# First batch's steps in another order, zero products between them, and another token layout for keys and v

## The chip, the cores and the metric

The kernel runs on one core of one Trainium2 chip. The metric is the device time of one execution in microseconds (us). Engines are named as in the profile: PE is TensorE (PEld its weight loads), DVE is VectorE, ACT is ScalarE, POOL is GpSimd, SP is SyncE. Each engine works through its own list of instructions in order and waits on semaphores for the others. SP issues the loads of q and k, POOL those of v and of the weights.

## What is computed

The reference is an attention with normalised q and k, followed by a two-layer network with a tanh-GELU; batch is 8, heads 12, sequence 448, head size 64, d_model 768, d_ff 2048.

```
def rmsnorm(x, g):
    rms = np.sqrt(np.mean(x * x, axis=-1, keepdims=True) + 1e-06)
    return x / rms * g
q_n, k_n = (rmsnorm(q, g_q), rmsnorm(k, g_k))
scores = scale * np.matmul(q_n, k_n.transpose(0, 1, 3, 2))
attn = np.exp(scores - np.max(scores, axis=-1, keepdims=True))
attn = attn / (np.sum(attn, axis=-1, keepdims=True) + 1e-09)
attn_out = np.matmul(attn, v)
x = attn_out.transpose(0, 2, 1, 3).reshape(B * S, H * D)
h = x @ w_in
g = 0.5 * h * (1.0 + np.tanh(c * (h + 0.044715 * h * h * h)))
out = g @ w_out
```

## The kernel before

**Tiling.** A batch's 12 heads are worked on as six pairs `hp`; two pairs with the same `c = hp // 2` are loaded together (a load chunk `(b, c)`, halves `j = hp % 2`). A chunk brings q of four heads with four tokens in a row on 112 places (partitions) and k of the same heads. The 448 keys of a head are cut into 3 tiles of 128 keys and a rest of 64. The rests of two heads share one tile: slot `NK = 3` of the seven slots of `rawk`, where head half 0 owns places 0 to 63 and head half 1 places 64 to 127 (`own(j)`). Of v the 3 full tiles lie in `vb`, the rests in `vr`, whose other half is zero. There is one `vb` and one `vr` for even and one for odd batches.

**Steps of a chunk.** Squares of q and k (`sq`, `sk`), their sums (`tq`, `tk`, DVE), the inverse root (`rs`, a Ln and an Exp on ACT), the normalised q and k (`nq`, `nk`), transposes on PE (`tpq`, `tpk`), and their copies to SBUF (`cq`, `ck`). A letter after a colon names the engine (A is ACT, D is DVE, P is POOL). Then for each of 21 score tiles the scores (`s0` to `s20`, PE) and their exponential (`e0` to `e20`, ACT, into `ex` or, for a tile of rests, `exr`); for each pair the sums over keys (`sa`, `sb`, PE with `ones`), the reciprocals (`st`, `rc`, `rb`, DVE), the product with v (`xa`, `xb`, PE) and its scaling (`xt`, DVE). `v0`, `v1`, `v2` are the v loads of batch 0, `V0` to `V2` those of batch 1, `w` and `o` the loads of the two weights, `L11` and `L12` load chunks of batch 1, all queued on POOL or SP at the place where they stand. Capital letters are steps of batch 1.

**What sets the order.** For the first batch the order is written out by hand in the string `FRONT`; `front()` issues one step after the other, and each engine sees its own steps in that order. The `mb`, `ma`, `mc`, `md` steps are the first network layer (`mm1`) of batch 0, `g` its GELU. Later batches run in a loop in which the scores of batch b+1 lie between the second-layer products (`mm2`) of batch b; this loop is not part of the change, except for the loads and the v products that it calls. The step `y` issues products of zeros with 224 columns and `z` such with 448 (`idle`), whose results nothing reads; the kernel begins with 20 of the latter. Score tiles have two places in PSUM, and a third after step `U`.

## Time and profile before

| | |
|---|---|
| median of 3 runs | 413.26 us (412.65 to 413.44) |
| the profiled execution's own time | 413.83 us |
| its span, first to last instruction | 412.1 us |
| mean granted TensorE clock | 0.992 |
| PE busy | 403.7 us (98%) |
| ACT, DVE, POOL busy | 296.2, 274.3 and 131.8 us |
| DMA moved | 54.21 MB in 97870 packets |

Busy time is the time in which an engine has an instruction in it. Matmuls overlap, so that PE can be busy while a matmul that could start is late. Idle time before an instruction is given in brackets with what ended it. The `PEclk` rows give the share of full clock that TensorE was granted.

### The profile page before, as it was taken

The page shows a single profiled execution, that of the slowest core. Times are in us where ns is not written, and L with a number is a line of the kernel's source. Part 1 is how long each engine was busy: PE and PEld are TensorE (multiplying, and loading weights), DVE is VectorE, ACT ScalarE, POOL GpSimd, SP SyncE. Part 2 cuts the span into 40 slices and gives each one's busy share as a digit, 9 for nine tenths or more (in the row PEclk, how much of TensorE's full clock was granted, in tenths as well). Part 3 has the DMA queues.
Part 4 walks back from the last instruction along what each step waited for, and adds up shares of the span by engine and source line. Part 5 has one row for each costly group of instructions (what it writes and reads, how often), then busy time and mean ns, then how long its engine had stood idle before and what let it go on. Part 6 is the DMA issues. An engine that isn't in the chain of part 4 may idle for free.

```text
span 412.1 us, 10085 instructions
## 1 busy us (share of the span) xinstructions
PE 403.7 (98%) x4207; PEld 243.5 (59%) x4207; DVE 274.3 (67%) x454; ACT 296.2 (72%) x398; POOL 131.8 (32%) x144
## 2 busy tenths in 40 slices
PE   8799999999999999999999999999999999999996
PEld 3344555566655666557655666556655575556664
DVE  4899739899899638884678747786488633783010
ACT  5797987969988587767977778785976558774300
POOL 7689000234500942037500745019310460000000
PEclk9699999999999999999999999999999999999999
DMA  8999995999981689229981399616991161210022
GB/s 191 227 235 228 203 196 141 227 227 192 213 145 38 139 176 207 66 52 176 222 140 41 78 203 171 136 40 145 171 145 40 23 112 40 72 46 2 2 77 78
DMA packets 97870, 54.21 MB, mean 132 GB/s; under 512 B 63776, under 2 KB 94368, under 8 KB 97824
## 3 DMA queue, kind: packets, MB, share of 16 engines
q1 hardware_dynamic: 71392, 41.69, 43.4%
q0 software_dynamic: 26112, 11.80, 22.5%
q8 instruction: 33, 0.54, 0.6%
q10 hardware_dynamic: 320, 0.07, 0.1%
q14 instruction: 13, 0.11, 0.1%
HBM read 45.61 MB, written 11.01 MB: 137 GB/s over the span
## 4 chain that ended last, share of the span: by engine, by line
PE 95%; SPq 2%; DMA 1%; DVE 0%; ACT 0%; issue 0%; ACTq 0%; DVEq 0%
PE o L441 36%; PE hh L412 31%; PE o L370 11%; PE sc L324 8%; PE h L412 5%; PE sc L310 1%; DMA rawq<-in_q_dram 1%; PE ox L370 1%; SPq L143 1%; SPq L118 1%; SPq L136 1%; PE tp L245 0%; PE o L477 0%; PE tp L238 0%; ACT ex L331 0%
## 5 line engine op out<-in xcount | busy, mean ns | idle before, releaser
L441 PE MATMUL o<-wout,g 128*64 128x384 bf16 (+1 forms) x1648 | 160.6, 327 | 0.0
L331 ACT ACTIVATE ex<-sc,shift 128x896 bf16<-128x896 f32 x144 | 136.1, 1011 | 1.3 <-PE sc L324 1.3
L412 PE MATMUL hh<-xT,win 128*64 128x448 bf16 (+1 forms) x1260 | 133.8, 353 | 0.0
L441 PEld LDWEIGHTS <-g 128*64 128x64 bf16 (+1 forms) x1648 | 96.2, 109 | 58.3 <-issue 14.8
L412 PEld LDWEIGHTS <-win 128*64 128x64 bf16 (+1 forms) x1440 | 95.4, 109 | 49.9 <-issue 3.2
L421 ACT ACTIVATE g<-hh 128x896 bf16<-128x896 f32 x56 | 50.1, 919 | 44.5 <-PE hh L412 44.4
L203 DVE TENSOR_REDUCE ss<-sq 128x14 f32<-128x896 f32 (+4 forms) x45 | 47.9, 1080 | 32.4 <-ACT sq L186 19.9
L454 ACT COPY osb<-o 128x384 f32<-128x384 f32 x50 | 24.2, 483 | 47.8 <-PE o L441 47.8
L788 POOL COPY mark<-es 1x1 bf16<-1x1 bf16 x8 | 1.8, 225 | 162.9 <-DVE es L345 158.5
L377 DVE STREAM_TRANSPOSE st<-o 128x448 f32<-128x448 f32 x48 | 31.1, 648 | 23.6 <-PE o L370 23.2
L324 PE MATMUL sc<-qT,kT 64*128 64x448 bf16 (+1 forms) x372 | 39.6, 360 | 1.7 <-DVE kT L264 1.3
L345 DVE TENSOR_TENSOR es<-ex 128x896 bf16<-128x896 bf16 x42 | 26.8, 637 | 12.0 <-ACT ex L331 12.0
L226 POOL TENSOR_TENSOR nrmq<-rawq,rinv 112x512 bf16<-112x512 f32 x33 | 34.0, 1043 | 0.0
L226 POOL TENSOR_TENSOR nrmk<-rawk,rinv 128x512 bf16<-128x512 f32 (+1 forms) x33 | 31.1, 957 | 4.2 <-ACT rinv L212 4.2
L385 DVE STREAM_TRANSPOSE rb<-rc 128x448 f32<-128x448 f32 x48 | 31.0, 645 | 1.6
L370 PE MATMUL o<-ex,vb 128*64 128x448 bf16 x252 | 30.9, 352 | 0.0
L279 DVE TENSOR_SCALAR kT<-kT,gcol 128x896 bf16<-128x896 bf16 x19 | 21.1, 1108 | 11.7 <-DMA kT<-nrmk 11.7
L343 DVE TENSOR_TENSOR es<-es,exr 64x896 bf16<-64x896 bf16 x42 | 25.9, 617 | 2.4 <-ACT exr L331 1.0
L345 DVE TENSOR_TENSOR es<-es,ex 128x896 bf16<-128x896 bf16 x42 | 25.5, 608 | 2.3 <-ACT ex L331 0.3
L395 DVE TENSOR_TENSOR xT<-o,rb 128x448 bf16<-128x448 f32 x42 | 25.8, 615 | 1.4 <-PE o L370 0.9
L188 POOL TENSOR_TENSOR sq<-rawq 112x1024 f32<-112x1024 f32 x9 | 17.0, 1893 | 28.4 <-DMA rawq<-in_q_dram 25.0
L324 PEld LDWEIGHTS <-kT 64*128 64x128 bf16 (+1 forms) x372 | 10.9, 99 | 24.6 <-issue 18.1
(83 smaller groups left out, 349.4 us busy)
## 6 DMA issues: line engine op xcount, KB each, us to landing
rawq<-in_q_dram SPq DMA_DIRECT2D x48, 224.0 KB, 4.4
rawk<-in_k_dram SPq DMA_DIRECT2D x48, 192.0 KB, 4.6
vb<-in_v_dram POOLq DMA_DIRECT2D x8, 576.0 KB, 10.1
win<-in_moe_w_in_dram POOLq DMA_DIRECT2D x4, 768.0 KB, 14.1
wout<-in_moe_w_out_dram POOLq DMA_DIRECT2D x4, 768.0 KB, 20.4
out_dram<-osb SPq DMA_DIRECT2D x7, 336.0 KB, 4.3
out_dram<-osb SPq DMA_DIRECT2D x8, 288.0 KB, 2.7
out_dram<-osb SPq DMA_DIRECT2D x8, 240.0 KB, 2.6
```

The source lines that it names most:

```text
L203: nc.vector.reduce_sum(stat(ssq[b % 3], b, c, n, j), view(n, sqs[n, b, c], j), axis=AX.X)
L226: eng.tensor_mul(dst.rearrange("p t a d -> p a t d"), view(n, raws[n, b, c], j), r.to_broadcast(list(r.shape) + [D]),)
L324: nc.tensor.matmul(sc[o, a, :S], kT[r, c, 4 * j + t, o], qT[b][r, hp], start=True, stop=True,)
L331: nc.scalar.activation(dst, sc[:, :, :S], AF.Exp, scale=scale, bias=shift)
L343: nc.vector.tensor_add(es[p], es[p], exrs[b, hp // 2][p])
L345: nc.vector.tensor_add(es, ex[:, 0] if t == 1 else es, ex[:, t])
L370: nc.tensor.matmul(o[a * D:(a + 1) * D], w(a), e[:, a], start=(i == 0), stop=(i + 1 == len(steps)),)
L377: nc.vector.transpose(oas["st"].rearrange("p a b -> p (a b)"), oas[0])
L385: nc.vector.transpose(oas["rb", hp], oas["rc"].to_broadcast([128, S // 32, 32]))
L412: nc.tensor.matmul(h[i * m:(i + 1) * m, j, :S], win[:, c // 2 + NCH * (c % 2), f * 128 + i * m:f * 128 + (i + 1) * m], xT[b][:, c], start= ...
L421: nc.scalar.activation(g[:, fs[0]:fs[0] + len(fs), (b % 2) * S:(b % 2 + 1) * S], hs1[fs[0]][:, :, :S], AF.Gelu_apprx_tanh)
L441: nc.tensor.matmul(o[j * m:(j + 1) * m, :HD], g[:, f, i * 128 + j * m:i * 128 + (j + 1) * m], wout[:, f, half * HD:(half + 1) * HD], start ...
```

## The change

Three things change together. First, k and v of a head are laid out anew: the first 256 tokens lie four in a row on the head half's own 64 places, the other 192 three in a row on the other 64 places. Slot 3 holds the fourth tokens of the own places, so that score tiles keep their shapes. A chunk's k comes in four transfers to 64 places each, where there were two to 128 places and two small ones to 64, and in another order. `vr` is gone: `vb` has a fourth slot, whose unused half is set to zero, and a batch's v comes in four transfers to 64 places instead of one to 128 and two small ones. The step `v0` now issues two transfers, `v1` and `v2` one each. Second, the order in `FRONT` changes, and some steps change their engine (`nk1` goes from DVE to POOL, `sq4` from POOL to ACT; of batch 1, `Sk2` and `Sq2` leave ACT for POOL and DVE, `Cq0` and `Ck0` change places between ACT and DVE, and `Sk1` stands ahead of `e20`). `v0` and `w0` are issued later, after the square `sk4`. Third, zero products are put into `FRONT`: `y4`, `z3`, `y3`, `z3`, `z1`, `y4`, `z1`, that is 11 of 224 columns and 8 of 448, where there was one `y3`.

```diff
@@ -93,8 +93,8 @@
     win = wts.tile([128, HP, d_ff], BF16)
     wout = wts.tile([128, nf, d_model], BF16)
 
-    vb = [wts.tile([128, H, NK, D], BF16, name=f"vb{i}") for i in range(2)]
-    vr = [wts.tile([128, 2, HP, D], BF16, name=f"vr{i}") for i in range(2)]
+
+    vb = [wts.tile([128, H, NK + 1, D], BF16, name=f"vb{i}") for i in range(2)]
     ones = consts.tile([128, D], BF16)
     onesr = consts.tile([128, 2, D], BF16)
     kT = consts.tile([128, NCH, NS, 128], BF16)
@@ -111,9 +111,13 @@
     def head(c, j):
         return 2 * c + HP * j
 
+    def raw_q(b, c):
+        if ("q", b, c) not in raws:
+            raws["q", b, c] = rawqk.tile([P, CH, NQ, D], F32, tag="rawq", name="rawq")
+        return raws["q", b, c]
+
     def load_q(b, c):
-        t = rawqk.tile([P, CH, NQ, D], F32, tag="rawq", name="rawq")
-        raws["q", b, c] = t
+        t = raw_q(b, c)
         return [
             lambda j=j: nc.sync.dma_start(
                 t[:, 2 * j:2 * j + 2],
@@ -122,7 +126,10 @@
             for j in range(2)
         ]
 
-    SM = 128 * NK
+    SM = 64 * (NK + 1)
+
+    def keys(j, n):
+        return (own(j), slice(0, SM)) if n > NK else (own(1 - j), slice(SM, S))
 
     def own(j):
         return slice(64 * j, 64 * j + 64)
@@ -131,33 +138,29 @@
         t = rawqk.tile([128, 2, NS, D], F32, tag="rawk", name="rawk")
         raws["k", b, c] = t
 
-        def main(j):
+        def part(j, n):
+
+            at, span = keys(j, n)
+            s = slice(NK * j + j * (n == NK), NK * j + j * (n == NK) + n)
             h = head(c, j)
             nc.sync.dma_start(
-                t[:, :, 4 * j:4 * j + NK],
-                k[b, h:h + 2, :SM].rearrange("a (p t) d -> p a t d", t=NK),
+                t[at, :, s], k[b, h:h + 2, span].rearrange("a (p t) d -> p a t d", t=n)
             )
-
-        def last(j):
-            h = head(c, j)
-            nc.sync.dma_start(t[own(j), :, NK], k[b, h:h + 2, SM:].rearrange("a p d -> p a d"))
-        return [lambda: main(0), lambda: main(1), lambda: last(0), lambda: last(1)]
+        return [lambda j=j, n=n: part(j, n) for j in range(2) for n in (4, 3)]
 
     def loads(b, c):
         lq, lk = load_q(b, c), load_k(b, c)
-        for go in (lq[0], lk[0], lq[1], *lk[1:]):
+        for go in (lq[0], *lk[:2], lq[1], *lk[2:]):
             go()
 
     def load_v(b, part):
-        if part == 0:
+
+        for j, n in ((0, NK), (1, NK)) if part == 0 else ((part - 1, NK + 1),):
+            at, span = keys(j, n)
+            first = j * (n == NK)
             nc.gpsimd.dma_start(
-                vb[b % 2].rearrange("p h t d -> p h (t d)"),
-                v[b, :, :SM].rearrange("h (p t) d -> p h (t d)", t=NK),
-            )
-        else:
-            j = part - 1
-            nc.gpsimd.dma_start(
-                vr[b % 2][own(j), j], v[b, HP * j:HP * j + HP, SM:].rearrange("h p d -> p h d")
+                vb[b % 2][at, HP * j:HP * j + HP, first:first + n].rearrange("p h t d -> p h (t d)"),
+                v[b, HP * j:HP * j + HP, span].rearrange("h (p t) d -> p h (t d)", t=n),
             )
 
     def view(n, t, j=None):
@@ -355,8 +358,12 @@
         o = oas[what]
         main = [exs[b, hp][:, t] for t in range(NK)]
         if what:
-            steps = [(main[t], lambda a, t=t: vb[b % 2][:, head(c, j) + a, t]) for t in range(NK)]
-            steps.append((exrs[b, c], lambda a: vr[b % 2][:, j, 2 * c + a]))
+            steps = [
+                (e, lambda a, t=t: vb[b % 2][:, head(c, j) + a, t])
+                for t, e in enumerate(main[:NK * (1 - j)] + [exrs[b, c]] + main[:NK * j])
+            ]
+            if j:
+                steps.append(steps.pop(0))
         elif b == 0:
             steps = [(e, lambda a: ones) for e in main] + [(exrs[b, c], lambda a: onesr[:, j])]
         else:
@@ -605,7 +612,6 @@
     nc.scalar.preload_act_table_set(EXP_SET)
     loads(0, 1)
     loads(0, 2)
-    loads(1, 0)
     nc.vector.memset(eps, 1e-6)
     nc.vector.memset(ones, 1.0)
     nc.vector.memset(rows, 1.0)
@@ -614,7 +620,8 @@
     for j in range(2):
         nc.gpsimd.memset(onesr[own(j), j], 1.0)
     for i in range(2):
-        nc.gpsimd.memset(vr[i], 0.0)
+        for j in range(2):
+            nc.gpsimd.memset(vb[i][own(1 - j), HP * j:HP * j + HP, NK * (1 - j)], 0.0)
     for i in range(1, 3):
         nc.gpsimd.memset(ssq[i], 1.0)
 
@@ -732,6 +739,9 @@
             w_out_part(i // 2, slice(i % 2 * nf // 2, (i % 2 + 1) * nf // 2))
         elif name == "L":
             loads(*divmod(i, 10))
+        elif name == "H":
+
+            eng.memset(raw_q(*divmod(i, 10))[:1, 0, 0, :1], 0.0)
         elif name in ("Sq", "Sk"):
             square(1, i, n, eng)
         elif name in ("Tq", "Tk"):
@@ -759,18 +769,18 @@
             raise ValueError(step)
 
     FRONT = """
-        sq0:A sk0:P gcol tq0 tk0 sq1:P rs0 sk1:A nq0:P v1 nk0:D shift tq1 tk1 sq2:A tpq0 tpk0 v2
-        v0 sk2:A rs1 sq3:A cq0:D ck0:D tq2 s0 e0 y3 s1 nk1:D nq1:D L11 e1 tpk1 tpq1 s2 sk3:P w0
-        tq3 tk2 rs2 e2 ck1:D cq1:D s3 e3 sa0 s4 sk4:P tk3 nq2:D nk2:D rs3 tpk2 tpq2 s5 sb0 tk4
-        ck2:D cq2:D nq3:D st0 e4 nk3:P e5 s6 sk5:P L12 e6 tpk3 tpq3 s7 e7 s8 sa1 s9 sb1 xa0 e8
-        sq4:P sq5:P w1 rc0 cq3:D rb0 ck3:D tq4 tk5 rs4 e9 xb0 s10 st1 xt0 rc1 rb1 tq5 e10 sa2
-        s11 e11 rs5 nk4:P nq4:P w2 nk5:P nq5:P xa1 xb1 sb2 s12 e12 s13 tpk4 tpq4 xt1 st2 ck4:D
-        cq4:D rc2 xa2 e13 rb2 sa3 xb2 s14 tpk5 tpq5 s15 e14 xt2 ck5:D cq5:D sb3 e15 U s16 s17
-        xa3 xb3 s18 w3 o0 Sk0:P e16 st3 rc3 rb3 e17 xt3 e18 s19 sa4 xa4 sb4 xb4 Tk0 st4 rc4 s20
-        mb0 mb1 mb2 mb3 sa5 e19 e20 o1 Sq0:P Sq1:P V0 rb4 GELU xt4 Tq0 xa5 sb5 xb5 st5 V1 V2 o2
-        o3 Sk1:A rc5 rb5 ma1 mc0 mc1 xt5 md0 ma2 md1 mc2 md2 Tq1 Tk1 g0 EXP md3 Rs0 g1 Nk00:D
-        Nq11:D Nq00:D Tp0 md4 Cq0:A g2 Sq2:A g3 Nk10:D Nk01:D Nq01:D Ck0:D Tp1 md5 Sk2:A Tq2 Tk2
-        Nk11:D Nq10:D Ck1:A g4 Cq1:A g5 md6 md7 g6 g7 md8 g8
+        L10 sq0:A gcol tq0 sk0:P tk0 rs0 sq1:P sk1:A nq0:P nk0:D v1 tq1 shift tk1 sq2:A y4 tpk0
+        tpq0 z3 v2 sk2:A rs1 sq3:A ck0:D cq0:D s0 e0 s1 nq1:D nk1:P L11 e1 tpq1 y3 s2 tpk1 z3
+        sk3:P tq3 tq2 cq1:D tk2 ck1:D e2 rs2 z1 s3 e3 tk3 nk2:D nq2:D rs3 s4 y4 z1 sa0 s5 tpq2
+        sb0 tpk2 nq3:D st0 cq2:D ck2:D e4 sk4:P v0 nk3:P e5 s6 sk5:P w0 sq5:P w1 L12 e6 sa1 tpq3
+        s7 s8 tpk3 sb1 sq4:A e7 s9 xa0 e8 tk4 rc0 cq3:D rb0 ck3:D st1 rc1 tq4 e9 rs4 xb0 s10 xt0
+        rb1 tq5 tk5 e10 sa2 s11 xa1 xb1 e11 rs5 w2 nq4:P nk4:P nq5:P nk5:P sb2 tpq4 s12 s13 tpk4
+        xt1 st2 e12 cq4:D rc2 ck4:D xa2 e13 rb2 xb2 sa3 s14 tpq5 tpk5 e14 xt2 cq5:D ck5:D s15
+        sb3 e15 U s16 s17 xa3 xb3 s18 w3 Sk0:P e16 st3 rc3 rb3 e17 xt3 e18 s19 sa4 sb4 xa4 xb4
+        s20 Tk0 st4 rc4 mb0 mb1 mb2 mb3 sa5 e19 Sk1:A o0 o1 Sq0:P Sq1:P V0 V1 rb4 e20 GELU xt4
+        Tq0 xa5 sb5 xb5 st5 V2 o2 o3 Sk2:P rc5 rb5 mc0 ma1 mc1 xt5 md0 ma2 md1 mc2 md2 Tk1 Tq1
+        g0 EXP md3 Rs0 g1 Nk00:D Nq00:D Nq01:D Tp0 md4 Sq2:D Ck0:A g2 Tq2 Cq0:D Nk11:D g3 Nk10:D
+        Nk01:D Nq11:D Tk2 Nq10:D g4 md5 Tp1 g5 Ck1:A Cq1:A md6 md7 g6 g7 md8 g8
 """
     for step in FRONT.split():
         front(step)
```

## The prediction

> **What bounds the kernel now.** I read the page first: the span, the shares of the engines, and the clock by slices (tenths of full clock in 40 equal slices of 10.3 us).
>
> ```profile
> span 412.1 us, 10085 instructions
> ...
> PE 403.7 (98%) x4207; PEld 243.5 (59%) x4207; DVE 274.3 (67%) x454; ACT 296.2 (72%) x398; POOL 131.8 (32%) x144
> ...
> PEclk9699999999999999999999999999999999999999
> ```
>
> PE is the bound with 98% of the span, and its clock is short in the second slice alone (the 6), which is where the change is. I therefore asked for busy time by stretches; the stretches are those of the granted clock (columns: busy time and count of PE, PEld, DVE, ACT, POOL, then granted clock, DMA share, GB/s).
>
> ```profile
> 7.18:14.00 6.82, 4.33 (x34) 2.05 (x32) 6.10 (x13) 4.71 (x8) 6.05 (x7) 1.00 1.22 228
> 14.00:20.83 6.83, 6.05 (x37) 2.45 (x36) 5.57 (x13) 5.67 (x9) 4.03 (x5) 0.50 1.37 230
> 20.83:27.66 6.83, 6.42 (x63) 2.96 (x62) 6.72 (x15) 6.51 (x11) 5.45 (x6) 1.00 1.17 243
> 27.66:34.49 6.83, 6.83 (x63) 3.12 (x60) 6.29 (x13) 6.53 (x8) 6.80 (x7) 1.00 1.20 227
> ```
>
> From 7.18 to 14.00 PE was busy for 4.33 of 6.82 us (63%); in the 6.83 us behind that the clock was 0.50. After 20.83 it is full again, and PE is nearly always busy. So two things cost time: waits before 14, and half clock up to 20.83. The timeline of PE shows both (start, us, instruction, and in brackets the idle time before it).
>
> ```profile
> 8.13 0.93 PE L217 MATMUL w<-zeros 128*128 128x448 bf16 x4
> ...
> 10.73 0.36 PE L324 MATMUL sc<-qT,kT 64*128 64x448 bf16 x2 [1.30 <-DVE kT L264]
> 11.02 0.46 PE L217 MATMUL w<-zeros 128*128 128x224 bf16 x3
> 11.42 0.36 PE L324 MATMUL sc<-qT,kT 64*128 64x448 bf16 x2
> ...
> 13.36 0.37 PE L238 MATMUL tp<-ident,nrmq 112*128 112x112 bf16 x4 [1.05 <-DVE nrmq L226]
> ...
> 14.80 0.88 PE L310 MATMUL sc<-qT,kT 64*64 64x448 bf16 x4 [0.78 <-DVE kT L264]
> 15.62 0.96 PE L370 MATMUL o<-ex,ones 128*64 128x448 bf16 x4
> ...
> 22.14 0.36 PE L324 MATMUL sc<-qT,kT 64*128 64x448 bf16 x2 [0.41 <-ACT ex L331]
> 22.44 0.57 PE L370 MATMUL o<-ex,ones 128*64 128x448 bf16 x4
> ```
>
> The same four key sums take 0.96 us at 15.62 and 0.57 us at 22.44. The score tile at 22.14 (`s9`) is the last with a wait that the view shows, and it waits for ACT. Behind it PE is the bound to the end, so what makes `s9` earlier makes the end earlier, provided that ACT and DVE keep up. ACT up to there:
>
> ```profile
> 10.54 0.61 ACT L186 ACTIVATE g<-rawq 112x512 f32<-112x512 f32 x1
> 11.13 1.91 ACT L331 ACTIVATE ex<-sc,shift 128x896 bf16<-128x896 f32 x2
> 14.39 0.31 ACT L209 ACTIVATE lg<-ss,eps 128x14 f32<-128x14 f32 x1 [1.36 <-DVE ss L203]
> ...
> 18.40 1.01 ACT L331 ACTIVATE ex<-sc,shift 128x896 bf16<-128x896 f32 x1 [0.29 <-PE sc L324]
> 19.77 1.01 ACT L331 ACTIVATE ex<-sc,shift 128x896 bf16<-128x896 f32 x1 [0.37 <-PE sc L324]
> 21.09 1.90 ACT L331 ACTIVATE ex<-sc,shift 128x896 bf16<-128x896 f32 x2 [0.31 <-PE sc L324]
> ...
> 28.68 2.80 ACT L331 ACTIVATE ex<-sc,shift 128x896 bf16<-128x896 f32 x3 [0.30 <-PE sc L324]
> ```
>
> From the first exponential at 11.13 ACT stands still for 1.36 us, waiting for a DVE sum, and three times for PE at half clock: 0.29 + 0.37 + 0.31 = 0.97 us. The rest is work, so ACT allows `s9` to come at most 1.36 + 0.97 = 2.33 us earlier.
>
> **The change part by part.**
>
> *Zero products.* Eleven of 224 columns at (11.42 − 11.02) / 3 = 0.13 us and eight of 448 at 0.93 / 4 = 0.23 us make 1.4 + 1.8 = 3.2 us of PE, less the 0.4 us of the `y3` that was there: 2.8 us. They stand where PE waits: `y4` and `z3` around the first transposes (the gap of 1.30), `y3`, `z3`, `z1` around those of the second pair (1.05), `y4`, `z1` before the first key sums (0.78). These three gaps and the 0.41 are 3.54 us, so I cost the products at nothing. If the gaps close because the new order is better, the products stand in the way of work; at the worst that is the 2.8 us, but ACT, not PE, ends the last wait, and PE would first use up its slack. Their use is the clock: the gaps in 7.18 to 14.00 were 2.49 us, and five of the seven groups (`y4` and `z3` with 1.2 us, `y3`, `z3` and `z1` with 1.3 us) fall there, so PE's busy share goes from 63% to about (4.33 + 2.5 − 0.4) / 6.82 = 94%. That is like the 94% of the stretch 20.83 to 27.66 (6.42 of 6.83), behind which the clock stayed full. I take it that the clock stays full, and ACT's three waits go: −0.97 us. PE itself would gain half of 6.05 us, 3.0 us, but ACT then ends the wait.
>
> The Trainium skill, page "TensorE: Matmul & The Clock Gate", Part 1, states that the clock falls back after an idle window of some 3.4 us. The longest gap ahead of the drop was 1.30 us, so by this sentence the clock would not have fallen here at all; the trace differs, and it decides. By that rule the clock term would be nothing, and the sum below 0.97 us higher.
>
> *Order.* ACT's wait of 1.36 us was for the sums of the third half chunk, behind DVE's other work: DVE was busy 6.10 of 6.82 us. The new order takes `nk1` from DVE to POOL and puts `e2` ahead of `rs2`, so that ACT has an exponential to do meanwhile. I count −1.36 us, with 0 as the other end. `sq4` moves from POOL to ACT, ahead of `e7` and so ahead of `s9`: one square, 11.13 − 10.54 = +0.59 us. The wait of 0.30 us at 28.68 came at full clock and stays.
>
> *v and its queue.* `v0` is issued behind `sk4` and no longer ahead of `sk3`. It is needed by `xa0`, directly behind `s9`.
>
> ```profile
> 8.43 1.48 POOL L159 DMA_DIRECT2D vr<-in_v_dram  x2
> ...
> 13.62 0.84 POOL L188 TENSOR_TENSOR g<-rawk 128x384 f32<-128x384 f32 x1
> ```
>
> The answers on the two tiles of v and on rawk give issue times and landings (`vr` first, then `vb`, then the issue of k on SP, in ns):
>
> ```profile
> DMA to landing us min/median/max: 5.8/6.0/6.2
> ```
> ```profile
> DMA to landing us min/median/max: 10.7/14.6/18.5
> ```
> ```profile
> L136 SPq DMA_DIRECT2D rawk<-in_k_dram x6: 458/458/511, 1.2 to 9.3; - x6
> L143 SPq DMA_DIRECT2D rawk<-in_k_dram x6: 601/607/751, 2.8 to 11.0; - x6
> ```
>
> `sk4` ends at 14.46 before; in the new order `v0` is issued about there. With the 5.8 us of `vr` the half that `xa0` needs lands at 20.3; with the 10.7 us of `vb`, at 25.2. `xa0` would be due 0.3 us behind `s9`, at about 22.14 − 1.74 + 0.3 = 20.7. `v1` and `v2` are issued at about 8.4 as before, so little is queued ahead. The half has three times the bytes of one `vr` transfer (three tokens on 64 places against one) and a quarter of those of `vb`, so it is nearer to the lower end; for its larger size I add 0.7 us, which lands it at 21.0 and makes a wait of 0.3 us (0 to 4.5).
>
> *k in four transfers.* Issue on SP: two transfers to 128 places (0.458 each) and two to 64 (0.607) become four to 64, +0.30 us per chunk, beside transfers that keep the DMA engines full (share 1.22); the fourths of tokens, 256 bytes each before, ride in longer rows. I book nothing; the bounds are +0.3 and −0.3 us, since only the first chunk is on the path. The Trainium skill, page "DMA: Bandwidth & Descriptors", section "Rules for kernel authors", advises one transfer to 128 partitions over two to halves, because the halves serialise; by that rule the sum would be 0.3 us higher. No row here shows it.
>
> *Later batches.* One more v issue on POOL per batch, about 0.7 us, where POOL waits long:
>
> ```profile
> POOL mark L788 <- DVE es L345: 158.5, 7, 36.1
> ```
>
> The row sums POOL's idle time before the step that stands ahead of the v loads in seven batches, up to 36.1 us in one. With that cover gone the last v transfer would be issued 0.7 us later (1.48 / 2, from the row at 8.43). The v products have the same shapes. `o2` and `o3` are issued behind one more v transfer on POOL, `Sk2` is queued behind them, and DVE's `Tk2` waits for it, with `Nq10` behind that. These serve the third chunk of batch 1, whose scores come after all of the first layer, so I book nothing; without that cover it is a square, which takes 0.84 us for 384 columns and so some 2 us for 896.
>
> **Sum.** −0.97 − 1.36 + 0.59 + 0.30 = −1.44 us. The profiled execution took 413.83 us (span 412.1 and 1.73 around it), giving 412.4; the median of the runs is 0.57 us lower, 413.26, giving 411.8 us.
>
> **The rivals.** *The clock falls all the same, later.* The new products end at the first key sums, while a stretch after them, such as 14.00 to 20.83, holds transposes, score tiles and waits for ACT, and from there on PE depends on ACT with a share that may be near the 63% that was too little. If the drop starts at 14, ACT's waits stay (+0.97) and the last two groups (4 × 0.13 + 0.19 = 0.7 us) take twice as long (+0.7): 411.8 + 1.7 = 413.5. If it starts at 20.83, where PE has no slack, half clock takes half of the 6.42 us of work, less the 0.41 us in which PE was idle there: 411.8 + 2.8 = 414.6, slower than before. It decides when the busy share of one such stretch ends between 63% and 94%, which no run here has yet bracketed closer. For it: I cannot place the stretches in another run. Against it: the products close the largest gaps. The Trainium skill, same page, Part 4, says that transposes don't count as busy for the gate, and Part 1 that its window runs free; the first would help this rival, and no run here shows either. Chance 0.22.
>
> *v0 is late.* The transfer shares the DMA engines with the loads of batch 1, and `xa0` waits up to 4.5 us instead of 0.3. 412.5 to 416, most likely 413. For it: DMA share over 1 throughout; against: a small transfer with little queued ahead. Chance 0.08.
>
> *DVE takes the place of ACT.* DVE is busy 6.72 of 6.83 us after 20.83, and its list is little shorter; then the 1.36 us are not got and only the clock's part is left: 411.8 + 1.36 = 413.2, no change. Chance 0.12.
>
> **How the numbers follow.** Forecast 0.58, its own range 411.0 to 412.4 (below, ACT's limit less the square, 2.33 − 0.59 = 1.74, and 0.3 of the k transfers give 411.2, and the three runs scatter by 0.4 to each side; above, 0.6 for v and k). The range reaches past the clock's milder case and DVE's: 411.0 to 414.2. A difference of 0.2%, 0.83 us, is what can be told from none: faster means below 412.4, slower above 414.1. Faster gets the forecast and a little of the others, 0.60; the same gets DVE, most of the late v and half of the drop at 14, 0.22; slower the later drop and the worst of v, 0.18.
>
> **What would show it.** Right: granted clock 1.00 from 7 us on, no idle ACT between `rs2` and `e7`, `s9` near 20.4. Wrong: a stretch at 0.50 after the zero products (first rival); idle PE before the first `ox` with a v transfer as releaser (second); ACT waiting for DVE sums or PE for copies to `kT` (third).

## The result: slower by 1.2%, mostly because v comes late and the clock falls behind that wait

| | before | changed |
|---|---|---|
| median, us | 413.40 (412.65 to 413.72, 6 runs) | 418.05 (416.17 to 419.74, 6 runs) |
| ratio, with its 95% interval | | 1.0117 (1.0097 to 1.0137) |
| the profiled execution, us (span) | 413.83 (412.1) | 418.05 (416.3) |
| DMA packets | 97870 | 85710 |
| POOL busy, us | 131.8 | 136.0 |

The forecast was 411.8 us, in 411.0 to 414.2. The measured time lies beyond the upper end of the range: the change made the kernel slower and not faster.

The page of the changed kernel: the same bound, and the short slice of the clock is now the third and no longer the second.

```profile
span 416.3 us, 10151 instructions
...
PE 405.6 (97%) x4223; PEld 244.4 (59%) x4223; DVE 273.4 (66%) x454; ACT 295.1 (71%) x397; POOL 136.0 (33%) x155
...
PEclk9969999999999999999999999999999999999999
```

Busy time by stretches of the granted clock (columns as in the prediction):

```profile
5.13:14.00 8.87, 7.45 (x54) 3.68 (x52) 6.72 (x16) 6.68 (x14) 7.26 (x7) 1.00 1.01 214
14.00:22.20 8.20, 5.84 (x52) 2.48 (x48) 6.67 (x15) 7.67 (x12) 5.58 (x7) 1.00 1.19 206
22.20:29.03 6.83, 5.20 (x28) 1.95 (x30) 2.39 (x5) 2.95 (x6) 3.99 (x6) 0.50 1.23 218
```

The clock stays full to 22.20, as forecast up to there. PE is busy for 84% of the first stretch (7.45 of 8.87); in the forecast's own stretch, 7.18 to 14.00, it is busy for 5.40 of 6.82 us, 79% where 94% was forecast. Then come 6.83 us at half clock. The timeline of PE shows what stands at their head:

```profile
20.67 0.36 PE L327 MATMUL sc<-qT,kT 64*128 64x448 bf16 x2
23.83 1.33 PE L377 MATMUL ox<-ex,vb 128*64 128x448 bf16 x6 [2.79 <-DMA vb<-in_v_dram]
...
25.98 0.96 PE L377 MATMUL o<-ex,ones 128*64 128x448 bf16 x4
...
37.26 0.36 PE L419 MATMUL hh<-xT,win 128*128 128x448 bf16 x1
...
56.61 0.35 PE L419 MATMUL h<-xT,win 128*128 128x448 bf16 x1
```

The same places before:

```profile
22.84 0.36 PE L370 MATMUL ox<-ex,vb 128*64 128x448 bf16 x2
...
33.94 0.36 PE L412 MATMUL hh<-xT,win 128*128 128x448 bf16 x1
...
52.49 0.35 PE L412 MATMUL h<-xT,win 128*128 128x448 bf16 x1
```

The first line is `s9`: 20.67 instead of 22.14, so it does come 1.47 us earlier (1.74 was forecast). The account of the profiled span then runs: −1.47 at `s9`; from `s9` to the first product with v 3.16 us instead of 0.70, +2.46; from there to the first tile of the first layer, the first `hh`, 13.43 instead of 11.10, +2.33; on to `h` 19.35 instead of 18.55, +0.80; from there to the end 359.66 instead of 359.56, +0.10. The sum is +4.2, the difference of the spans.

The chain of waits names the way to the late v (start, us, what):

```profile
9.68 6.84 DMA rawk<-in_k_dram
16.53 0.07 issue
16.59 0.77 POOL g L191
17.36 6.33 DMA vb<-in_v_dram
23.69 0.14 issue
23.83 0.55 PE ox L377
```

A transfer of k lands at 16.53; the square `sk4` on POOL waits for it; `v0` is queued behind that square and is issued at 17.36; its first half lands at 23.69, and PE starts. POOL's timeline shows it standing still meanwhile:

```profile
12.23 1.03 POOL L191 TENSOR_TENSOR g<-rawk 128x512 f32<-128x512 f32 x1
16.59 0.82 POOL L191 TENSOR_TENSOR g<-rawk 128x384 f32<-128x384 f32 x1 [3.33 <-DMA rawk<-in_k_dram]
17.36 1.36 POOL L161 DMA_DIRECT2D vb<-in_v_dram  x2
```

Before, `sk4` waited for nothing. It needed one transfer of k, the second of its chunk, issued at 8.29 and landed 4.8 us later. In the new layout it needs two, the second and the third. The third is issued at 9.68 and takes 6.8 us. These are the answers on rawk for those two issues, before and changed:

```profile
L136 SPq DMA_DIRECT2D rawk<-in_k_dram x1: 458/458/458, 8.3 to 8.3; - x1
...
DMA to landing us min/median/max: 4.8/4.8/4.8
```
```profile
L146 SPq DMA_DIRECT2D rawk<-in_k_dram x1: 605/605/605, 9.7 to 9.7; - x1
...
DMA to landing us min/median/max: 6.8/6.8/6.8
```

Two of the kernels below part the two causes. POOL's `sk4` with the new layout and the old order, and then with the old places and the new order:

```profile
16.96 0.82 POOL L191 TENSOR_TENSOR g<-rawk 128x384 f32<-128x384 f32 x1 [2.83 <-DMA rawk<-in_k_dram]
```
```profile
13.93 1.36 POOL L188 TENSOR_TENSOR g<-rawk 128x384 f32<-128x384 f32 x1 [1.25 <-DMA rawk<-in_k_dram]
```

So the new layout made `sk4` late, and the new order had put `v0` behind `sk4`. The late `sk4` also holds back `nk3`, which stands behind it and `v0` on POOL: PE waits 1.01 us for that at 19.84, ahead of `s9`.

### The profile page after: what moved, and what is told of

The parts are those of the page before. It is cut to its first block, busy times and chain, and to the rows that moved or that the text cites. A ratio compares the mean times of both kernels' runs of the same rounds, so it can differ in the third digit from the quotient of the medians.

```text
span 416.3 us, 10151 instructions
## 1 busy us (share of the span) xinstructions
PE 405.6 (97%) x4223; PEld 244.4 (59%) x4223; DVE 273.4 (66%) x454; ACT 295.1 (71%) x397; POOL 136.0 (33%) x155
## 2 busy tenths in 40 slices
DMA packets 85710, 54.21 MB, mean 130 GB/s; under 512 B 45472, under 2 KB 82208, under 8 KB 85664
## 4 chain that ended last, share of the span: by engine, by line
PE 91%; DMA 3%; SPq 2%; DVE 2%; ACT 1%; issue 1%; POOL 0%; ACTq 0%; DVEq 0%
PE o L448 36%; PE hh L419 28%; PE o L377 11%; PE sc L327 8%; PE h L419 5%; DMA rawk<-in_k_dram 2%; PE ox L377 2%; DMA vb<-in_v_dram 2%; SPq L146 1%; PE sc L313 1%; DVE nrmq L229 1%; SPq L122 1%; PE o L484 0%; DVE nrmk L229 0%; ACT L759 0%
## 5 line engine op out<-in xcount | busy, mean ns | idle before, releaser
L384 DVE STREAM_TRANSPOSE st<-o 128x448 f32<-128x448 f32 x48 | 31.1, 647 | 22.4 <-PE o L377 22.2
L229 POOL TENSOR_TENSOR nrmk<-rawk,rinv 128x512 bf16<-128x512 f32 (+1 forms) x34 | 32.5, 971 | 0.6 <-ACT rinv L215 0.6
L377 PEld LDWEIGHTS <-vb 128*64 128x64 bf16 x384 | 22.2, 112 | 16.3 <-issue 4.3
L282 DVE TENSOR_SCALAR kT<-kT,gcol 128x896 bf16<-128x896 bf16 x19 | 19.8, 1043 | 12.0 <-DMA kT<-nrmk 11.9
L334 ACT ACTIVATE exr<-sc,shift 128x896 bf16<-128x896 f32 x24 | 24.4, 1019 | 3.3 <-PE sc L313 3.3
```

Source lines behind the costliest of these rows:

```text
L229: eng.tensor_mul(dst.rearrange("p t a d -> p a t d"), view(n, raws[n, b, c], j), r.to_broadcast(list(r.shape) + [D]),)
L334: nc.scalar.activation(dst, sc[:, :, :S], AF.Exp, scale=scale, bias=shift)
L377: nc.tensor.matmul(o[a * D:(a + 1) * D], w(a), e[:, a], start=(i == 0), stop=(i + 1 == len(steps)),)
L384: nc.vector.transpose(oas["st"].rearrange("p a b -> p (a b)"), oas[0])
```

## The experiments

Each ratio is against runs of the kernel before on the same chip, in the same session; the medians of before were 412.94 to 413.28 us there. The names in the table are explained below, each with its edit; in the order of steps, "..." stands for steps that stay.

| kernel | median, us (range) | ratio to before (95%) |
|---|---|---|
| `v0` ahead of `sk4` | 414.94 (412.60 to 416.40) | 1.0044 (1.0024 to 1.0064) |
| layout alone | 414.80 (413.79 to 415.82) | 1.0044 (1.0028 to 1.0060) |
| no zero products | 416.06 (415.09 to 417.78) | 1.0079 (1.0057 to 1.0101) |
| old tail | 417.74 (416.74 to 419.50) | 1.0119 (1.0097 to 1.0141) |
| `v0` ahead of `sk4`, q second | 412.98 (412.10 to 414.66) | 1.0004 (0.9991 to 1.0017) |
| `v0` ahead of `sk4`, old places from batch 2 | 413.58 (411.51 to 415.18) | 1.0013 (0.9996 to 1.0030) |
| `v0` behind `nk1`, old tail | 413.13 (412.17 to 415.02) | 1.0010 (0.9996 to 1.0024) |
| new order on the kernel before | 414.78 (413.42 to 415.33) | 1.0043 (1.0030 to 1.0056) |
| held loads, new places | 414.09 (412.76 to 415.76) | 1.0022 (1.0009 to 1.0035) |
| filled wait | 415.76 (414.47 to 416.88) | 1.0061 (1.0044 to 1.0078) |
| zero products on the kernel before | 413.29 (411.78 to 416.48) | 1.0009 (0.9988 to 1.0031) |
| held loads, old places, new order | 412.14 (411.94 to 412.75) | 0.9979 (0.9968 to 0.9990) |
| held loads, old places from batch 2 | 413.12 (412.45 to 414.00) | 0.9997 (0.9984 to 1.0010) |
| held loads, new places from batch 2 | 413.34 (412.83 to 414.12) | 1.0002 (0.9991 to 1.0012) |
| held loads, old places, old order | 412.01 (410.90 to 412.77) | 0.9966 (0.9954 to 0.9979) |
| held loads, new places, again | 413.69 (412.31 to 414.27) | 1.0005 (0.9993 to 1.0017) |
| the old-order one without zero products | 412.56 (411.89 to 414.21) | 0.9992 (0.9979 to 1.0005) |

### Is it v0's place in POOL's queue?

```diff
-... e4 sk4:P v0 nk3:P ...
+... e4 v0 sk4:P nk3:P ...
```

> One step is moved: v0 stands directly ahead of sk4 on POOL's list, no longer directly behind it. Theory (v0 is late because it queues behind a square that itself waits for a k transfer, and the 2.79 us that PE then waits let the clock fall to half on a PE with no slack): v0 is issued at about 13.3 us instead of 17.36, its first half lands near 19.6, the wait ahead of the first v product is under 0.5 us, no stretch at half clock follows it, hh0 comes at 31 to 33 us instead of 37.26, and the time is 412.0 to 414.0. Rival A (the clock falls at that place all the same, since the busy share there is too low even without the wait): the wait goes but the half-clock stretch stays, 414.5 to 416. Rival B (the wait belongs to the DMA engines and not to the place in POOL's list): v0 lands at 23 us again, 417 to 419.

One step changed places with its neighbour, and 3.1 us of the 4.65 came back (3.0 by the ratios). The timeline of PE:

```profile
21.07 0.76 PE L377 MATMUL ox<-ex,vb 128*64 128x448 bf16 x6 [0.73 <-DMA vb<-in_v_dram]
...
24.31 0.76 PE L377 MATMUL ox<-ex,vb 128*64 128x448 bf16 x6 [0.88 <-DMA vb<-in_v_dram]
...
33.22 1.69 PE L419 MATMUL hh<-xT,win 128*128 128x448 bf16 x8
```

The wait of 2.79 became two of 0.73 and 0.88, one for each half of the heads, and the granted clock is full to 412.47, a moment after the last instruction. `hh` begins at 33.22 instead of 37.26. So the theory holds, but the landing was misjudged by 1.3 us (20.93 instead of 19.6) and the median lies 1 us above the range. The trace is of one of the shorter executions: in four of the twelve runs the mean clock was 0.996, which is some 3.3 us at half clock (0.004 × 412 × 2), and three others took 415.65 to 416.36 us at full clock. What those lose, this trace does not show.

One step further up, here with the old order behind `s18` as well:

```diff
-... nq1:D nk1:P ... sk3:P ... sk4:P v0 ...
+... nq1:D nk1:P v0 ... sk3:P ... sk4:P ...
```

> The changed kernel with v0 directly behind nk1, ahead of sk3 and sk4, and the old order behind s18. With v0 ahead of sk4 its halves landed at 20.93 and 24.26 us and PE still waited 0.73 and 0.88 us. Theory: v0 issued at 12.2 us lands its halves at about 19.9 and 22.6, both waits go, hh0 near 31.8 us, and the time is 1.4 us below that of the kernel with v0 ahead of sk4: 413.0 to 414.0. Rival (SP's k transfers of the second and third chunk, and sk3 behind the issue, come later by as much): 414.5 to 415.5, with PE waiting for a sum or a square instead.

Both waits for v are gone and 413.13 is in the range, but its rival came in part too: `sk3` behind the longer queue starts 1.5 us later, and PE waits 1.21 us for a normalised q at 17.30. `hh` is at 33.35, not 31.8.

### The wait or the clock?

```diff
-... e7 s9 xa0 ...
+... e7 s9 y20 xa0 ...
```

> The changed kernel as it is, with twenty more zero products of 224 columns directly ahead of the first v product, 2.6 us at 0.13 each, in the wait for v0. They compute nothing that is used. Theory (of the 3 us that a late v0 costs, some 2 us come not from the wait but from the half clock that follows it): v0 lands at 23.7 as before, no half clock follows, hh0 near 35.2 us instead of 37.26, 415.5 to 416.5 against 418. Rival (the clock falls for the share before the wait): 418, half clock from about 22 us on as before. A second rival (the loss is the wait alone): half clock goes and the time stays at 418.

```profile
20.76 2.09 PE L220 MATMUL w<-zeros 128*128 128x224 bf16 x20
23.18 0.76 PE L377 MATMUL ox<-ex,vb 128*64 128x448 bf16 x6 [0.33 <-DMA vb<-in_v_dram]
...
34.45 0.36 PE L419 MATMUL hh<-xT,win 128*128 128x448 bf16 x1
```

Products that nobody reads, put where nothing could be done anyway, give 2.3 us of the median (415.76 against 418.05). v lands at 23.05 in this profile, little earlier than without them, but no half clock follows, and from the first v product to the first `hh` it takes 11.27 us instead of 13.43. So of the price of the late v about 2 us are the clock behind it, and the rest is the wait.

```diff
-... y4 tpk0 tpq0 z3 ... y3 s2 tpk1 z3 ... z1 ... y4 z1 sa0 ...
+... tpk0 tpq0 ... e0 y3 s1 ... s2 tpk1 ... sa0 ...
```

> The changed kernel without its new zero products (the seven groups y4, z3, y3, z3, z1, y4, z1 are out, one y3 stands behind e0 as in the kernel before). Theory (v0 late): v0 still lands at 23.7 us, the wait of about 2.8 us stays or is shorter by what PE comes later; the drop to half clock comes earlier, at about 14 us, where PE has slack, and not behind the wait; so 415 to 417.5, a little faster than the changed kernel. Rival D (the zero products stand in the way of work and are themselves the loss): 413.5 or less. Rival E (they do what they are for and save a second drop): 419 or more.

416.06, 2 us less than with the zero products (1.6 by the ratios), which agrees with the theory's number. The wait for v was still 1.95 us, because PE itself came later. In its profile the clock fell to half twice, from 12.98 for 6.83 us and from 23.22 for 3.41 us. So without zero products the first fall comes where PE has slack, as before, and the second is shorter.

### Does the layout cost anything by itself?

```diff
-        L10 sq0:A gcol tq0 sk0:P tk0 rs0 sq1:P sk1:A nq0:P nk0:D v1 tq1 shift tk1 sq2:A y4 tpk0
+        L10 sq0:A sk0:P gcol tq0 tk0 sq1:P rs0 sk1:A nq0:P v1 nk0:D shift tq1 tk1 sq2:A tpq0
...
```

(and so on to the end: the order before, with its one `y3`)

> The new places of k and v with the old order of steps and its single y3, no other zero products; v0 is therefore issued ahead of sk3 again. Theory (the layout costs nothing, all of the loss is in the order): 413.0 to 414.2, no difference from the kernel before, half clock near 14 to 21 us as before. Rival C (the 64-place transfers are slower, on the first path and in all later batches): 415 or more, with k or v as releaser in waits of PE or POOL that the kernel before does not have.

It costs 1.9 us, so my theory that it is free falls. Its profile shows no wait for v and no single large gap; `hh` is 0.3 us later than before, and 0.35 us more are lost after 240 us. That is 0.7 of the 1.9 us; the rest stays open. Half clock lasts 10.24 us instead of 6.83 there, but mean clocks of 0.986 to 0.992 occur in runs of both kernels, so that this is not the layout's doing. Two experiments with `v0` ahead of `sk4` looked into the later batches. The first restores the old place of the second q transfer:

```diff
-        for go in (lq[0], *lk[:2], lq[1], *lk[2:]):
+        for go in (lq[0], lk[0], lq[1], *lk[1:]) if b > 1 else (lq[0], *lk[:2], lq[1], *lk[2:]):
```

> The changed kernel with v0 ahead of sk4, and from batch 2 on the old order of issue for a chunk: the second q transfer stands behind one k transfer and no longer behind two; the transfers themselves are the new ones. Theory (later batches: the second q transfer of the third chunk is issued 0.8 us later than before, POOL's two squares start later, DVE's sum behind them waits and PE has a gap of 0.6 to 0.9 us in a batch here and there): POOL's square of q starts earlier by up to 0.6 us, PE has no gap over 0.15 us after 60 us or one less, 413.5 to 414.5 against the 414.94 of the kernel with v0 ahead of sk4 alone. Rival (the squares wait for k, not q, and the k transfers take 0.7 us more of issue): 414.9, no change.

The second gives the batches from 2 on the old transfers of k, and likewise of v, into the new tiles (`old` issues one transfer):

```diff
+        if b >= 2:
+            first, rest = slice(0, 128 * NK), slice(128 * NK, S)
+            return [lambda j=j: old(j, slice(0, 128), first, slice(4 * j, 4 * j + NK)) for j in range(2)] + [
+                lambda j=j: old(j, own(j), rest, slice(NK, NK + 1)) for j in range(2)]
```

> The changed kernel with v0 ahead of sk4, and from batch 2 on the old places of k and v, so three tokens at all 128 places and the rest in transfers of one token; batches 0 and 1 keep the new places. Theory (the new places cost 0.3 to 0.9 us in later batches, in the third chunk of a batch, and nothing in the first): 412.5 to 413.8, no gap of PE over 0.15 us after 60 us. Rival (the loss of the layout lies in batch 0, where the first chunks land later): 414.9, no change.

Against the 1.0044 of `v0` ahead of `sk4` alone, q second gave 1.0004, more than expected. The old places gave 1.0013, as expected. But in both kernels v's second half still landed at 24 to 25 us, with waits of 1.36 and 1.75, and the runs stayed 2.6 and 3.7 us apart, so that they don't separate layout from luck with v. For that the wait for v had to go.

### The layout again, with v in time

The unused step `H` clears one element of a load's buffer, and the load has to wait for that. It holds the loads of batch 1, issued from 10.3 us on ahead of `v0`, though their data serves only from 30 us on:

```diff
-        L10 sq0:A gcol ... L11 e1 ... e4 sk4:P v0 nk3:P ...
+        sq0:A gcol ... e1 ... e4 v0 H10:P L10 L11 sk4:P nk3:P ...
```

(with q second, and the old order behind `s18`)

> The changed kernel with v0 ahead of sk4, the old issue order of q from batch 2 on, the old order behind s18, and the loads of batch 1's first two chunks held back: GpSimd clears one element of their buffer behind v0, so that they are issued at about 14.5 us and no longer from 10.3 us on, ahead of v0. Theory (the second half of v0, at 24.05 us in the kernel with q second, shares the DMA engines with loads that nobody needs before 30 us): its halves land near 19 and 21 us, the wait of 1.36 us goes, hh0 at 31.5 to 32 us instead of 33.0, 411.2 to 412.2, faster than both kernels. Rival (the held loads now meet the input weights, which the first layer needs at 32.4 us): a wait for weights or for batch 1's squares takes the place, 412.5 to 414.

v's halves landed at 19.34 and 20.67, the clock stayed full, and `hh` came at 32.39. The profiled run took 412.76 us, 1.1 less than the profiled run of before. But it was the shortest of twelve, and the median was 414.09, slower than before. That left open where the other runs lose. Four more kernels ask it, with the places mixed by batch. The first has old places throughout, v's big transfer in two halves, and `v0` directly behind `v2`:

```diff
-        if b >= 2:
+        if b >= 0:
-... y4 tpk0 tpq0 z3 v2 sk2:A ... L11 ... sk3:P ... sk4:P v0 ...
+... y4 tpk0 tpq0 z3 v2 v0 sk2:A ... sk3:P H10:P L10 L11 ... sk4:P ...
```

> The old places of k and v in all batches (v's big transfer as two, one for each half of the heads) with the new order and its zero products up to s18, the old order behind it, v0 directly behind v2, and the loads of batch 1's first two chunks held back behind sk3. Theory (the new order is worth its 1.4 us once v is in time): v0's halves land at about 17 and 20 us, no wait for v, full clock, hh0 at 31.5 to 32.5 us, 411.3 to 412.3. Rival (the order is worth nothing; another wait takes its place): hh0 at 33.5 us or later, 413 or more.

The second is the kernel with the held loads and new places, with `if b >= 2` in it:

> The kernel with the held loads (v0 ahead of sk4, batch 1's first two chunks held back, old order behind s18), with the old places of k and v from batch 2 on; batches 0 and 1 keep the new places. Theory (the held-load kernel, 414.1 at full clock with runs from 412.8 to 415.8, loses 1 to 3 us in some runs by the new places in batches 2 to 7): 412.0 to 412.8 with runs within 1 us. Rival (the loss comes from the new places in batches 0 and 1, their loads and the products of the first chunks): 413.5 to 414.5, runs as far apart as before.

The third is the one with old places, its condition turned round:

```diff
-        if b >= 0:
+        if b < 2:
```

> The reverse: the kernel with old places, new order and held loads (412.14), with the new places of k and v from batch 2 on, q second in each chunk. Theory (later batches lose by the new places): 413.5 to 414.5 with runs up to 3 us apart, PE waiting in the trace for DVE in some batch after 240 us. Rival (the loss lies in batches 0 and 1): 412.0 to 412.8.

The fourth is the kernel with held loads and new places once more, as it was:

> The kernel with the held loads and the new places once more, unchanged, on the same chip as the three others: 413.5 to 414.5 is expected with runs 2 to 3 us apart at full clock. If the trace falls on one of the long runs, theory: the missing time shows as gaps of PE behind DVE in batches 2 to 6; rival: as gaps before 60 us.

Old places in all batches gave 412.14; new ones from batch 2 on 413.34, new ones in the first two batches 413.12, new ones in all 413.69 and 414.09. Each part costs about 1 us, and neither theory alone holds: I had expected 412.0 to 412.8 for the kernel with old places from batch 2, and the kernel with new places from batch 2 stayed just under its range, with runs 1.3 us apart and not 3. By the ratios the later batches cost 0.23% (0.9979 to 1.0002), the first two 0.18%, and both together 0.26% and 0.43% in the two measurements, 1.1 and 1.8 us. The first two batches' part is not purely layout, since `v0` stands at another place there; in the trace with old places from batch 2 PE waits 1.07 us at 24.69 for a normalised q on POOL. Nor is it in every trace: the last of the four has its first `hh` at 31.75, the kernel with old places at 32.07.

For the later batches the trace of the last of these four kernels shows the place. POOL, DVE and PE while the scores of batch 5 run:

```profile
246.12 1.89 POOL L191 TENSOR_TENSOR sq<-rawq 112x1024 f32<-112x1024 f32 x1 [7.38 <-DMA rawq<-in_q_dram]
248.53 2.81 POOL L191 TENSOR_TENSOR sq<-rawk 128x896 f32<-128x896 f32 x1 [0.51 <-DMA rawk<-in_k_dram]
```
```profile
248.05 1.22 DVE L206 TENSOR_REDUCE ss<-sq 112x16 f32<-112x1024 f32 x1 [4.21 <-POOL sq L191]
249.19 0.61 DVE L348 TENSOR_TENSOR es<-ex 128x896 bf16<-128x896 bf16 x1
249.90 1.92 DVE L348 TENSOR_TENSOR es<-es,ex 128x896 bf16<-128x896 bf16 x1
...
253.57 1.09 DVE L206 TENSOR_REDUCE ss<-sq 128x14 f32<-128x896 f32 x1
254.57 0.64 DVE L384 STREAM_TRANSPOSE st<-o 128x448 f32<-128x448 f32 x1
```
```profile
255.26 0.76 PE L377 MATMUL o<-ex,vb 128*64 128x448 bf16 x6 [0.81 <-DVE st L384]
```

With old places (held loads, old places, new order) the same two squares:

```profile
245.43 1.90 POOL L210 TENSOR_TENSOR sq<-rawq 112x1024 f32<-112x1024 f32 x1 [6.50 <-DMA rawq<-in_q_dram]
247.28 1.68 POOL L210 TENSOR_TENSOR sq<-rawk 128x896 f32<-128x896 f32 x1
```

And the answers on rawk for that chunk's four transfers of k, new places and then old:

```profile
L146 SPq DMA_DIRECT2D rawk<-in_k_dram x4: 605/606/616, 240.8 to 243.4; - x4
...
DMA to landing us min/median/max: 4.1/4.6/5.4
```
```profile
L152 SPq DMA_DIRECT2D rawk<-in_k_dram x4: 463/539/612, 240.2 to 242.4; - x4
...
DMA to landing us min/median/max: 3.7/4.1/4.7
```

Four transfers to 64 places take 0.4 us more of SP's time from the first to the last issue (2.6 against 2.2), and 0.5 us more to land. The square of k waits 0.51 us for them and starts 1.25 us later; the square of q ahead of it was already 0.69 us late. Then it falls beside DVE's additions of the exponentials: the square takes 2.81 us instead of 1.68, and the addition 1.92 us. In the kernel with old places the square was nearly over when they began, and an addition of this form took 0.63. The next sum, DVE's transpose and PE's product with v all queue behind, and PE stands for 0.81 us. From batch 4's to batch 5's second layer this run loses 1.3 us against the one with old places; the run with new places from batch 2 on loses 1.4 us there, and the first run of the held loads nothing. That it happens in some executions and not in others, since the two lists slide against each other by fractions of a us, is inferred from these runs.

The pair is not bound to the new places, though. It also stands, one batch later, in the traces of two kernels of a later section that have old places throughout (held loads and old order, with and without zero products). POOL and DVE in the one with zero products:

```profile
295.64 3.22 POOL L210 TENSOR_TENSOR sq<-rawk 128x896 f32<-128x896 f32 x1
```
```profile
297.43 1.92 DVE L367 TENSOR_TENSOR es<-es,ex 128x896 bf16<-128x896 bf16 x1
```

Here the square of k did not wait for k at all; PE stood for 0.39 us behind it (0.51 in the kernel without zero products), and the batch took 0.6 and 0.7 us more. Such a wait of PE is in five of the eleven traces with new places in the later batches, and in two of the eight with old ones. So the stretched pair is shown, and the price of the new places there, about 1 us, is measured over many runs; that the later landing of k is what brings the pair about is not shown.

The Trainium skill, page "GPSIMD Engine Reference", section "1. Specifications", says that GpSimd shares its SBUF interfaces with VectorE and contends with DVE instructions that read two inputs from SBUF. The rows agree: 2.81 for 1.68 and 1.92 for 0.63, on both sides of one overlap. No run here moved one of them away by itself.

### The tail of batch 1

```diff
-        sb3 e15 U s16 s17 xa3 xb3 s18 w3 Sk0:P e16 st3 rc3 rb3 e17 xt3 e18 s19 sa4 sb4 xa4 xb4
+        sb3 e15 U s16 s17 xa3 xb3 s18 w3 o0 Sk0:P e16 st3 rc3 rb3 e17 xt3 e18 s19 sa4 xa4 sb4
...
```

(and so on to the end: the order before)

> The changed kernel with the old order of everything behind s18 (squares, sums and norms of batch 1, the last v and output-weight loads, the first layer's start); up to s18 nothing differs. Theory: the delay grows from 3.3 us at hh0 to 4.1 us at the last h tile because the norms of batch 1 wait for Sk2 on POOL and a slow pair of norms on DVE; with the old tail these 0.8 us go: 416.8 to 417.6. Rival F (the 0.8 us are the same late start carried on, and not a matter of the tail's order): 418, no change.

No change in the median. In its profile the stretch from the first `hh` to `h` is indeed shorter, 18.54 us instead of 19.35 (56.70 − 38.16), as before the change, but v happened to land later (a wait of 3.51). So the 0.8 us are real within the trace and too small to be told from the scatter of v's landing. In the trace of the changed kernel they come from DVE's timeline:

```profile
46.80 2.90 DVE L229 TENSOR_TENSOR nrmq<-rawq,rinv 112x512 bf16<-112x512 f32 x2
49.61 1.21 DVE L191 TENSOR_TENSOR sq<-rawq 112x1024 f32<-112x1024 f32 x1
```

Two products that take 0.68 each elsewhere took 2.90 beside POOL's square (47.44 to 49.13), and a square that ACT did before stands behind them. The product with k that PE needs came 0.64 us late. The new tail does not always cost this: with `v0` ahead of `sk4` and the same tail the stretch from `hh` to `h` is 18.55 us, and the two products take 1.28.

### What the zero products and the order are worth

```diff
-... tpq0 tpk0 v2 ... e0 y3 s1 ... tpk1 tpq1 s2 ... rs2 e2 ... e3 sa0 ...
+... y4 tpq0 tpk0 z3 v2 ... e0 s1 ... y3 tpk1 tpq1 z3 s2 ... rs2 z1 e2 ... e3 y4 z1 sa0 ...
```

> The kernel before, in its places and order, with the seven groups of zero products at the like places (around the first and the second pair of transposes, behind rs2, ahead of the first key sums) in place of its one group. Theory of the forecast: the clock stays full past 14 us and 0.97 us of waits go, 412.2 to 412.5 against 413. Rival (half clock in that stretch costs next to nothing because ACT and the loads set the pace there): 413, no change, with full clock. Second rival (the clock falls later, on a PE without slack): 414 or more.

No change in the median, with the forecast's mechanism (full clock past 14 us) and the second rival of this experiment, the later fall, side by side. In the profiled run the clock was full from 4.51 on and fell at 21.58, for 3.41 us. PE waited there for v, issued at 9.65 and landed at 21.98:

```profile
22.02 1.33 PE L370 MATMUL ox<-ex,vb 128*64 128x448 bf16 x6 [2.10 <-DMA vb<-in_v_dram]
```

Of the twelve runs the eight with a mean granted clock of 0.998 or more took 411.78 to 413.37 us, the four with 0.992 to 0.996 414.40 to 416.48. So these products make PE earlier, PE then runs into the landing of v, and whether that wait costs the clock decides the time.

On the kernel before, the changed order, with `v0` where it stood:

```diff
-... v2 sk2:A ... sk4:P v0 ...
+... v2 v0 sk2:A ... sk4:P ...
```

> The kernel before, with its places of k and v, and the changed order with its zero products; v0, here one transfer of three tokens to 128 places, stands directly behind v2 as it did. Theory (order and zero products do what was forecast, and the layout and the late v took it back): v0 lands near 21 us, the wait for it is under 1 us, the clock stays full, hh0 at 32 to 33 us, 411.3 to 412.6 against the kernel before's 412.9 to 413.4. Rival (the order brings nothing even on the old places): 413 or more.

The median, 414.78, is in the rival's range, and the trace has the same wait as the one above: 2.45 us for v at 21.73, and 3.41 us at half clock from 22.50 on. `s9` was early, at 18.92 (19.06 with the zero products alone and the old order), and v was not. With the hold, v in time and old places, order and zero products can be told apart.

The next kernel is the one with held loads, old places and new order, with the order before up to `s18` as well, and zero products in it:

```diff
+... y4 tpq0 tpk0 z3 v2 v0 ... y3 tpk1 tpq1 z3 ... sk3:P H10:P L10 L11 ... z1 ... y4 z1 sa0 ...
```

> Old places, old order with the zero products, v's big transfer in two halves, and batch 1's first two chunks held back behind sk3; against the kernel with the new order (412.14) only the order up to s18 differs. Theory (the new order is worth what was forecast for it once nothing waits for v: 1.36 for the wait of ScalarE, less 0.59 for sq4, so 0.8 us): hh0 near 32.9 us instead of 32.07, 412.7 to 413.3. Rival (the hold and the split of v are the gain, the order is worth nothing): 412.0 to 412.4.

And the same without them:

```diff
-... y4 tpq0 tpk0 z3 ... y3 tpk1 tpq1 z3 ... rs2 z1 ... y4 z1 sa0 ...
+... tpq0 tpk0 ... e0 y3 s1 ... tpk1 tpq1 ... rs2 ... sa0 ...
```

> As the kernel with the old order and held loads (412.01), without its new zero products: old places, old order with its one y3, v's big transfer in two halves, batch 1's first two chunks held back behind sk3. Theory (the clock's part of the forecast is right where nothing waits for v: ScalarE's 0.97 us of waits at half clock): half clock near 14 to 21 us as in the kernel before, 412.8 to 413.4. Rival (the hold and the split are the whole gain): 411.8 to 412.3.

The old order gave 412.01, the new one 412.14 (0.9966 and 0.9979): the order up to `s18` is worth nothing here. The kernel with the new order had come out in its theory's range, but not for its theory's reason. Without zero products the median was 412.56, between the two ranges, and the ratio 0.9992, not to be told from the kernel before. Against 0.9966 with them that is 0.26%, 1.1 us; the ends of the two intervals touch, and by the medians it is 0.55 us, but the two ran on different chips, each against its own runs of before.

The traces agree that it is the clock. Without zero products half clock lasts from 11.32 to 21.56 us, ACT waits 0.51, 0.36 and 0.39 us for PE up to 20 us, and the first `hh` comes at 33.05. With them the clock stays full, one such wait of 0.20 us is left, and `hh` comes at 31.77. So of the 1.4 us by which the kernel with held loads, old places, old order and zero products is faster than the kernel before (0.9966, 0.9954 to 0.9979) most is the zero products, once v is in time.

## Why the prediction was wrong

A gain of 1.44 us was forecast, and the medians show a loss of 4.65.

**v and its queue: the step that failed.** I took `sk4`'s end at 14.46 from the trace of before and had `v0` issued "about there". It was issued at 17.36, because `sk4` had become late by the other half of the same change: its k now came as two transfers, the second landing at 16.53. The time from issue to landing was well guessed (6.33 us, against 5.8 plus 0.7). The wait was 2.79 us instead of 0.3, inside the bounds of 0 to 4.5. Moving `v0` ahead of `sk4` alone gave back 3.1 us, and filling the wait 2.3.

**Two rivals that are one.** I priced a late v as a wait (0.08) and a later fall of the clock as a matter of busy share (0.22), each alone. The filled wait shows that they belong together: the wait brings the fall, on a PE without slack, for 2 us more. Had I added the rival's 2.8 for a drop at 20.83 to a wait of 2.5, the time would have been 417.

**k in four transfers: 0 ± 0.3.** It is 1 to 1.9 us. The layout alone gave 1.9; the runs with v in time gave 1.1 and 1.8 for both parts together. The first part of the error is that I counted SP's issue time and not which transfer a square needs. The second is that I called later batches free: I looked at v's issues there and not at k's landing or at what POOL's square may run beside. Where in the later batches the loss arises is shown for one collision only, which old places have too. The Trainium skill, page "DMA: Bandwidth & Descriptors", section "Rules for kernel authors", had spoken against transfers to halves; the direction agrees, the price of the whole layout was several times the 0.3 that I gave it.

**Zero products: −0.97, right in size and wrong in its condition.** They kept the clock full up to 22.2, and are worth some 1.1 us by the ratios where v is in time. On the kernel before they are worth nothing, because PE, made earlier, meets the landing of v: in the profile of before it landed at 20.63, and PE needed it at 22.84; in that one it landed at 21.98, and PE had waited for 2.10 us. Why v itself took 12.3 us there instead of 10.7 stays open. I had bounded the gain of `s9` by ACT (2.33 us); the next bound behind it was v.

**Order: −1.36 + 0.59, not got.** ACT's wait of 1.36 us for a DVE sum is gone in the changed kernel, but it goes with the old order too:

```profile
12.57 0.31 ACT L209 ACTIVATE lg<-ss,eps 128x14 f32<-128x14 f32 x1 [0.18 <-DVE ss L203]
```
```profile
13.17 0.31 ACT L231 ACTIVATE lg<-ss,eps 128x14 f32<-128x14 f32 x1 [0.17 <-DVE ss L225]
```

These rows of ACT are from the zero products on the kernel before and from the old order with held loads; without zero products the latter has no such wait either. I had credited the order with a wait that the one profile of the kernel before shows; whether its other executions have it isn't known. And `s9`, which the order was to make earlier, came no later without it: 19.06 with the old order and 18.92 with the new one, both on the old places with zero products. So the zero products alone make `s9` earlier than the 20.67 of the changed kernel.

**Right:** `s9` at 20.67 (20.4 forecast), full clock to behind `s9`, ACT without its waits, and that the tail could cost something (0.8 us, of the "some 2 us" without cover). The last was luck: I had looked at a late `Sk2`, and what delayed DVE were products that took longer beside it.

## What to carry to other kernels

A load that is issued by a computing engine is as late as the instruction ahead of it in that engine's queue (`v0` went out at 17.36, behind a square that began at 16.59); when a change moves it behind a step, follow what that step waits for in the changed kernel, not in the old one. Price a new wait of PE together with the clock that may fall behind it, and look whether filling the wait is cheaper than removing it. Before a forecast adds up gains on the path, list the next landing that the earlier work will meet.

## What the runs showed of the hardware

Every stretch of the granted clock at half, between two at full, lasted 3.41, 6.83 or 10.24 us, one, two or three times 3.41. In the profiles waits of PE of 1.36 and 1.75 us left the clock at full, while those of 1.95, 2.10, 2.45, 2.79 and 3.51 us had half clock around their end. Yet it also came without any such wait, in the kernel before and in the ones without new zero products, where PE's work had many short gaps.

PE's busy share fits all of these better than the length of a wait. These are the 3.41 us ahead of the fall, in the kernel before and in the changed one, and the like stretch of the filled wait, behind which the clock stayed full:

```profile
10.59:14.00 3.41, 2.09 (x17) 0.93 (x17) 3.41 (x6) 2.45 (x4) 2.64 (x4) 1.00 1.32 223
```
```profile
18.79:22.20 3.41, 1.23 (x12) 0.46 (x10) 2.49 (x6) 2.94 (x4) 3.39 (x4) 1.00 1.25 202
```
```profile
18.96:22.37 3.41, 2.73 (x27) 2.08 (x28) 2.46 (x5) 3.09 (x4) 3.39 (x4) 1.00 1.30 219
```

PE was busy for 61%, 36% and 80% of them. Cut into such stretches, counted from the changes of the clock, the first 60 us of all nineteen traces say this: ahead of each of the nine falls PE was busy for 11 to 61% of a stretch; where full clock stayed, for 65% or more, but for two stretches with 56 and 61%. So in this kernel the limit lies near 60%, below the 63 to 94% within which the forecast's first rival had put it, and a wait of some 2 us can be enough to go under it. For the way back no such limit shows: two stretches at half clock with 93 and 95% were followed by another at half.

The Trainium skill, page "TensorE: Matmul & The Clock Gate", Part 1, gives a window of some 3.4 us that runs free. The lengths agree with that window; that it takes an idle one does not, since none of these waits but the one of 3.51 us was that long.
